# Two more early blocks, their stores on GpSimd's queue, and an operand loaded in two pieces

## The chip, the cores and the metric

The kernel runs on one core of a Trainium2 chip. The core has five engines with queues of their own: TensorE (PE in the profile; its weight loads are PEld), VectorE (DVE), ScalarE (ACT), GpSimd (POOL) and SyncE (SP). DMA transfers are issued by an engine's instruction, here mostly by SP, some by ACT and POOL, and are carried out by 16 DMA engines that all queues share. The metric is the time of one execution on the device in microseconds. The time before is 2615.43 us, the median of three runs.

## The reference

The kernel computes two things one after the other: a layer that mixes along the sequence by a Fourier transform, and a feed-forward layer on its result.

```python
X = np.fft.rfft(x, axis=1)                 # x: 8 x 3008 x 256
Yr = Xr @ w_r - Xi @ w_i + b_r
Yi = Xr @ w_i + Xi @ w_r + b_i
...                                        # soft threshold of Yr, Yi with 0.01
y = np.fft.irfft(Y, n=x.shape[1], axis=1)
...
h = y.reshape(24064, 256) @ w_in           # 256 x 2048
g = np.maximum(h, 0.0) ** 2
out = g @ w_out                            # 2048 x 256
```

## The kernel before

**Stages of the Fourier part.** 3008 is 64 x 47. Of each of the 8 batches, stage one transforms along the 47 in 13 blocks (J = 13): a block of 120 x 512 numbers of x is loaded, multiplied by constant matrices, copied from PSUM by ScalarE and stored in a scratch tensor `s1[b]` in HBM. Stage two reads `s1[b]` in 24 groups, transforms along the 64, mixes by w_r and w_i, applies the threshold, transforms back along the 64 and stores into `s3[b]`. The last stage (class `Back`) transforms back along the 47: it reads `s3[b]` in 16 groups per batch. Its operand is the tile `du`, 128 partitions x 3 x 256 numbers. Slots 0 and 1 are two columns of the first 128 rows of `s3[b]`; slot 2 holds on its lower and its upper 64 partitions the same two columns of the last 64 rows. `Back.mm` (lines 461, 464 and 465) multiplies slot 0, slot 1 and slot 2, in this order, for each half of 128 channels.

**Two phases.** In the first phase ("front") the first batch is done in full fp32 (`Fwd32`, `Unit32`), while the weights w_in and w_out are loaded and split into a high and a low part on VectorE, ScalarE and GpSimd. The second phase ("main") runs the feed-forward layer in steps of a tile's 500 or 504 tokens and 256 hidden units (class `Step`, line 484; psh and pso are its PSUM tiles): 7 products of a Strassen scheme on 128 x 250 tiles in three passes, the square of the positive part, a split, and 12 products with w_out. Between the steps' products the stages of later batches are spread by a list of jobs with due times in half steps, 96 to a batch (`fwd_tasks`, `pair_tasks`, `back_tasks`): the main phase of batch b also computes stage one of batch b + 2, stage two of batch b + 1 and the last stage for the next tile.

**The second batch** has no main phase ahead of it in which its stage one could run. The first `PRE` of its 13 blocks (class `Fwd2`, matmuls at line 352) are done at the end of the front: `load_early` issues their loads on SP, each behind the load of a stage two group, into buffers `x6`; after the last group `run` makes eight matmul passes, ScalarE copies 120 x 512 numbers to a buffer of tag `xf` (three of them), and the block is stored. Before, `PRE` is 5, and these stores are issued by ScalarE (line 225 on ACT). The other blocks run as jobs of the first main phase: the next two are loaded before its first step and due at 0.5 and 1.4, the rest at distances of 0.9; they are stored by SP. Stage two of the second batch is due from 10.6 on.

**What sets the order.** A planner orders each engine's instructions by its own estimate of times. `load_next` (line 108) chains all loads of the main phase in the order of the program on SP (and those of `kcm` on POOL). At the start of main the order is: the `du` loads of the first three groups, two weight loads (line 139), two `xt` loads for the next blocks of the second batch. The first three groups borrow the three `mc` buffers for `du`; all others share one buffer of tag `du`, so the load of a group can't start before the group ahead has been multiplied. The first tile's operands `yt` are made by VectorE and ScalarE out of the three groups' results (`dy`, `yr`, `ms`), and the main products (psh) need them.

Of the kernel before, what the change touches and what calls it, by code (L numbers as in the profile page):

```python
# [9 lines left out]
F32 = mybir.dt.float32  # L10
# [13 lines left out]
B, S, D, FF = 8, 3008, 256, 2048  # L24
N1, N2, G = 64, 47, 24
NP = N1 // 2
# [7 lines left out]
NP1 = N1 + 1  # L34
FRONT = {
    "a32": 1, "b32": 1, "w320": 1, "w321": 1, "big": 4, "small": 4, "ds": 1, "dw": 3, "ka": 5, "xe": 7,
    "kv": 3, "psf": 6, "x6": 5, "xf": 3, "nam": 1,
}
MAIN = {
    "xs": 1, "xe": 1, "du": 1, "kv": 1, "kp": 1, "kq": 1, "ksh": 1, "ksl": 1, "kxl": 1, "kb": 1, "yr": 1,  # L40
# [18 lines left out]
def fnet_moe(ctx: ExitStack, tc, x, w_r, w_i, b_r, b_i, w_in, w_out, bm, cm, dx, a32, c32, out):  # L59
    nc = tc.nc  # L60
    pe, act, dve, pool = nc.tensor, nc.scalar, nc.vector, nc.gpsimd
# [5 lines left out]
    s3 = [dram.tile([M2 + M2, NP, D], F32, name=f"s3_{b}") for b in range(B)]  # L67
# [13 lines left out]
    def memory(stack, name, **kwargs):  # L81
        return stack.enter_context(tc.tile_pool(name=name, bufs=2, reuse_waits="tile", **kwargs))
# [5 lines left out]
    def T(name, shape, dt, tag=None):  # L88
        tag = tag or name
        return pools.get(tag, phase["pool"]).tile(shape, dt, name=name, tag=tag, bufs=phase["bufs"].get(tag, 2))  # L90

    def bank(shape, name="psf"):
        return phase["psum"].tile(shape, F32, name=name, tag=name, bufs=phase["bufs"].get(name, 1))

    def copy(eng, out, in_):
        if eng is act:
            return act.copy(out=out, in_=in_)  # L97
        return eng.tensor_copy(out=out, in_=in_)  # L98
# [7 lines left out]
    def load_next(out, in_, eng=nc.sync):  # L106
        with tc.issue_after(chain[eng].ins):
            chain[eng] = eng.dma_start(out, in_)
# [24 lines left out]
    class Double:  # L133
# [3 lines left out]
        def load(self):  # L137
            self.st = T("dst", [128, 512, 2], I32, tag="big")
            self.get = nc.sync.dma_start(self.ins(self.st), self.src)
# [64 lines left out]
    class Fwd:  # L204
# [28 lines left out]
        def run(self):  # L233
            ps = bank([128, 2, D])
            for t in range(2):
                nc.tensor.matmul(ps[:M1, t], am32[:, t], self.u[:, t], start=True, stop=True)  # L236
            self.ev = T("xe", [M1, 1, 2, D], F32)
            copy(act, self.ev[:, 0], ps[:M1])
            self.store()
# [99 lines left out]
    class Fwd2(Fwd):  # L339
# [8 lines left out]
        def run(self):  # L348
            ps = bank([128, 2, D])
            for t in range(2):  # L350
                for i in range(2):
                    nc.tensor.matmul(
                        ps[:M1, t], nam if t and i else am32[:, t], self.xt[:, 0, i], start=i == 0, stop=i == 1
                    )
            self.ev = T("xe", [M1, 1, 2, D], F32, tag="xe" if self.q >= PRE else "xf")
            copy(act, self.ev[:, 0], ps[:M1])
            self.store(nc.sync if self.q >= PRE else act)

# [78 lines left out]
    class Back:  # L439
# [8 lines left out]
        def load(self):  # L448
            self.u = T("du", [128, 3, D], F32R, tag="du" if self.spans[0][0] else "mc")
            ps = slice(2 * self.q, 2 * self.q + 2)  # L450
            load_next(self.u[:, :2].bitcast(F32), s3[self.b][:128, ps])
            for p in range(2):
                load_next(self.u[64 * p:64 * p + 64, 2].bitcast(F32), s3[self.b][128:, 2 * self.q + p])

        def mm(self):
            self.y = y = T("dy", [128, 2, W2], F32)
# [190 lines left out]
    def convert(n, after=None):  # L647
        p = parts[n]
        p.bits(after)
        p.join()  # L650
        if n % 4 > 1:
            p.split()
        elif n % 4:
            win_sums(n // 4, parts[n - 1:n + 1])
# [8 lines left out]
    paced = [(n, 2 * (n - EARLY)) for n in range(EARLY, len(parts) - LATE)]  # L663
    loads = [(k - 1, parts[n]) for n, k in paced] + [(20 + j, p) for j, p in enumerate(parts[-LATE:-2])]

    PRE = 5
    nam = T("nam", [M1, M1], F32)
    act.mul(nam, am32[:, 1], -1.0)
    second = [Fwd2(1, q) for q in range(J)]
    for r in range(-5, len(units) + 3):  # L670
# [10 lines left out]
        while loads and loads[0][0] <= r:  # L681
            p = loads.pop(0)[1]
            with tc.issue_after((units[r + 5] if r + 5 < len(units) else units[-1]).get.ins):
                p.load()
        for n, k in paced:
            if k + 3 == r:
                convert(n, units[k])
        if 0 <= r - 12 < PRE:
            second[r - 12].load_early(units[min(r + 5, len(units) - 1)].get)
    for q in range(PRE):  # L690
        second[q].run()
# [3 lines left out]
        pool=memory(ctx, "main"), bufs={**{k: FRONT[k] for k in CONV}, **MAIN, "psf": 2}, psum=memory(ctx, "main_ps", space=PSUM)  # L695
# [16 lines left out]
    nam = T("nam", [M1, M1], F32)  # L712
    act.mul(nam, am32[:, 1], -1.0)
    for q in range(PRE, PRE + 2):
        second[q].load()
    jobs = []
    for m in range(2 * len(steps) + 4):
        b, r = divmod(m, slots)
        if r == 0 and b < B:
            jobs = [(t - slots, job) for t, job in jobs]  # L720
            if b + 1 < B:
                first, step, end = 1.0, 6.1, 7.1
                if b == 0:
                    first, step, end = 11.2, 5.3, 9.1
                    for q in range(PRE, J):
                        if q > PRE + 1:
# [112 lines left out]
```

## Time and profile before

| | |
|---|---|
| median of 3 runs | 2615.43 us |
| lowest and highest run | 2613.71 and 2618.53 us |
| the profiled execution | 2614.82 us, of which the span of its instructions is 2613.1 us |
| mean granted TensorE clock | 0.995 |
| TensorE busy | 2564.3 us, 98% of the span |
| matmuls of the steps (L484) | 1176.2 us (pso) and 1072.9 us (psh) |
| moved through DMA | 250.51 MB, 95 GB/s of HBM traffic over the span |

All numbers of the profile are of one execution. A row of the timeline gives the start and the length in microseconds, the engine, the line of the kernel, the operation, the tile written and the tiles read, and how many instructions are merged in the row; a bracket holds the idle time of the engine just before and what ended it. Rows with an engine name and q (SPq, ACTq, POOLq) are DMA issues: their time is that of the issue, and the transfer lands later. In the list of transfers a row gives the target and the source, the queue, the count, the size of one and the median time from issue to landing.

### The profile page before, as it was taken

To read this page: it belongs to the slowest core of one execution; us is meant where nothing else is said; L and a number is where in the kernel's file an instruction comes from. 1 tells how busy PE (TensorE), PEld (TensorE's weight loads), DVE (VectorE), ACT (ScalarE), POOL (GpSimd) and SP (SyncE) were. 2 spreads that over 40 slices of the span, in tenths; PEclk is the share of its full clock that TensorE was granted. 3 is DMA by queue.
4 is the path that set the end of the run, shared out by engine and by line. 5 is a ranking of instruction groups with operands and counts; after the bars stand their busy time and mean duration, and the time that the engine had idled before them with its cause. 6 is when DMAs were issued, how large, how long until landed. Compare 5 with 4: busy or idle time off the path is not lost.

```text
span 2613.1 us, 47540 instructions
## 1 busy us (share of the span) xinstructions
PE 2564.3 (98%) x16908; PEld 2347.0 (90%) x16908; DVE 1782.3 (68%) x3797; ACT 1672.7 (64%) x2434; POOL 1657.0 (63%) x1628
## 2 busy tenths in 40 slices
PE   6799999999999999999999999999999999999999
PEld 4689989999999999999999999999999999999998
DVE  6877766667767767577676776667676677765554
ACT  3556656666666666666666666666666666666665
POOL 2246666766766667667666676666667666666564
PEclk8999999999999999999999999999999999999999
DMA  8733332333332332233332333323332223221100
GB/s 267 236 110 110 102 113 82 95 106 107 95 91 75 116 104 86 84 95 113 104 92 82 97 110 100 99 76 101 103 108 80 71 79 101 71 65 41 33 17 17
DMA packets 191455, 250.51 MB, mean 96 GB/s; under 512 B 21755, under 2 KB 135923, under 8 KB 191219
## 3 DMA queue, kind: packets, MB, share of 16 engines
q1 hardware_dynamic: 178240, 223.89, 28.1%
q0 software_dynamic: 12304, 22.35, 3.6%
q8 instruction: 136, 2.23, 0.4%
q10 hardware_dynamic: 675, 1.23, 0.2%
q14 instruction: 100, 0.82, 0.1%
HBM read 146.85 MB, written 100.53 MB: 95 GB/s over the span
## 4 chain that ended last, share of the span: by engine, by line
PE 84%; POOL 1%; DMA 1%; issue 0%; DVE 0%; ACT 0%; POOLq 0%; SPq 0%; ACTq 0%; DVEq 0%
PE pso L484 36%; PE psh L484 32%; PE psf L301 6%; PE psf L280 2%; PE psf L236 2%; PE psf L333 2%; PE psf L464 1%; PE psf L465 1%; PE psf L461 1%; DMA du<-s 1%; POOL mg L101 0%; POOL yt L101 0%; POOL ms L101 0%; POOL ms L500 0%; ACT mc L484 0%
## 5 line engine op out<-in xcount | busy, mean ns | idle before, releaser
L101 POOL TENSOR_TENSOR mg<-mc,mg 128x500 fp32r<-128x500 f32 (+1 forms) x768 | 975.0, 1290 | 594.3 <-ACT mg L97 549.7
L484 PE MATMUL pso<-mg,wout 128*128 128x500 f32 (+1 forms) x4608 | 1176.2, 392 | 1.8 <-ACT mg L97 1.3
L484 PE MATMUL psh<-yt,win 128*128 128x250 f32 (+1 forms) x8064 | 1072.9, 281 | 1.5 <-DVE mc L484 1.2
L484 ACT ACTIVATE mc<-mc 128x1000 f32<-128x1000 f32 (+1 forms) x768 | 802.6, 1045 | 406.6 <-DVE mc L484 397.3
L484 PEld LDWEIGHTS psh<-yt,win 128*128 128x128 f32 x8064 | 1022.2, 189 | 34.3 <-PE psh L484 1.9
L484 PEld LDWEIGHTS pso<-mg,wout 128*128 128x128 f32 x4608 | 818.7, 189 | 130.0 <-POOL mg L101 1.9
L484 DVE TENSOR_TENSOR mc<-psh,mv 128x500 f32<-128x500 f32 (+3 forms) x768 | 419.1, 547 | 428.1 <-PE psh L484 395.4
L97 ACT CAST mg<-mc 128x1000 fp32r<-128x1000 f32 (+1 forms) x384 | 396.9, 1034 | 18.4 <-ACT mc L484 0.4
L484 DVE TENSOR_TENSOR mv<-psh,mu 128x500 f32<-128x500 f32 (+1 forms) x384 | 260.6, 679 | 53.5 <-PE psh L484 21.8
L301 PE MATMUL psf<-wx,kxh 128*128 128x256 f32 x1008 | 206.7, 281 | 2.4 <-ACT kxh L97 1.7
L98 DVE COPY mp<-psh 128x250 f32<-128x250 f32 (+1 forms) x384 | 159.7, 416 | 39.2 <-PE psh L484 16.2
L301 PEld LDWEIGHTS psf<-wx,kxh 128*128 128x128 f32 x1008 | 166.3, 189 | 6.7 <-ACT kxh L97 1.9
L101 POOL TENSOR_TENSOR ksl<-kv,ksh 128x512 fp32r<-128x512 f32 x84 | 108.8, 1295 | 94.6 <-ACT ksh L97 94.5
L484 DVE TENSOR_TENSOR mu<-psh,mp 128x250 f32<-128x250 f32 (+1 forms) x384 | 160.5, 418 | 11.5
L215 POOL TENSOR_TENSOR xs<-xt 120x256 f32<-120x256 f32 x156 | 115.4, 760 | 72.5 <-DMA xt<-x_in 67.6
L484 DVE TENSOR_TENSOR mc<-psh,mp 128x250 f32<-128x250 f32 (+1 forms) x384 | 156.8, 408 | 4.3 <-PE psh L484 2.8
L322 DVE TENSOR_TENSOR kv<-psf,ke 64x256 f32<-64x256 f32 x336 | 141.8, 422 | 22.9 <-PE psf L301 14.2
L301 PE MATMUL psf<-wx,kxl 128*128 128x256 f32 x504 | 141.1, 280 | 1.0 <-DVE kxl L101 1.0
L97 ACT COPY dy<-psf 128x188 f32<-128x188 f32 x256 | 76.9, 313 | 82.7 <-PE psf L465 82.2
L313 DVE TENSOR_TENSOR ke<-psf,bias 128x512 f32<-128x512 f32 x84 | 58.0, 691 | 102.0 <-PE psf L301 101.9
L97 ACT CAST ksh<-kv 128x512 fp32r<-128x512 f32 x84 | 52.0, 619 | 114.3 <-DVE kv L101 113.4
L97 ACT CAST kuh<-psf 128x256 fp32r<-128x256 f32 x192 | 68.4, 372 | 88.2 <-PE psf L333 71.4
(102 smaller groups left out, 2565.4 us busy)
## 6 DMA issues: line engine op xcount, KB each, us to landing
du<-s SPq DMA_DIRECT2D x128, 256.0 KB, 2.9
s<-kuh SPq DMA_DIRECT2D x192, 128.0 KB, 1.8
s<-kul SPq DMA_DIRECT2D x192, 128.0 KB, 1.8
kcm<-cm_in POOLq DMA_DIRECT2D x84, 256.0 KB, 3.3
ka<-s SPq DMA_DIRECT2D x84, 256.0 KB, 3.4
s<-xe SPq DMA_DIRECT2D x87, 240.0 KB, 2.4
xt<-x_in SPq DMA_DIRECT2D x86, 240.0 KB, 3.3
du<-s SPq DMA_DIRECT2D x256, 64.0 KB, 2.8
```

What stands on the lines that cost most here:

```text
L97: return act.copy(out=out, in_=in_)
L98: return eng.tensor_copy(out=out, in_=in_)
L101: return eng.tensor_tensor(out=out, in0=a, in1=b, op=ALU.subtract)
L215: return eng.tensor_tensor(out=out[:, :n], in0=self.xt[:, :n, 0], in1=self.xt[:, :n, 1], op=(ALU.add, ALU.subtract)[t])
L236: nc.tensor.matmul(ps[:M1, t], am32[:, t], self.u[:, t], start=True, stop=True)
L280: nc.tensor.matmul(pv[:, :, c, g, :], self.a[:, g, c * 128:(c + 1) * 128], bg, start=True, stop=True)
L301: self.last = nc.tensor.matmul(ps, l, wx[j][:, k, c, :], start=n == 0, stop=n == 5)
L313: dve.tensor_add(out=self.e, in0=self.pe, in1=bias)
L322: dve.tensor_add(out=v[64 * r:64 * r + 64, g], in0=ps[gs], in1=self.e[gs, r])
L333: nc.tensor.matmul(ps[:, :D], self.cm[:, g, j * 128:(j + 1) * 128], r[:, g], start=n == 0, stop=n == 2)
L461: mm = nc.tensor.matmul(pv[:, :, 0], self.u[:, 0, cs], dx_sb[:, 0], start=True, stop=False)
L484: last_of[eng] = op(*args, **kwargs)
```

## The change

It has three parts. `PRE` becomes 7, with 7 buffers of tag `x6`: blocks 5 and 6 of the second batch move from the main phase to the end of the front. Their place at the start of main, with the loads ahead of the first step, is taken by blocks 7 and 8, and the jobs of blocks 9 to 12 come two places (1.8) earlier. The stores of the early blocks are issued by GpSimd's queue. And slot 2 of `du` is loaded by one transfer of 128 partitions instead of two of 64: its HBM side is written by hand as 2 x 64 x 256 numbers (two columns, 64 rows, 256 channels), its SBUF side stays 128 x 256.

```diff
 FRONT = {
     "a32": 1, "b32": 1, "w320": 1, "w321": 1, "big": 4, "small": 4, "ds": 1, "dw": 3, "ka": 5, "xe": 7,
-    "kv": 3, "psf": 6, "x6": 5, "xf": 3, "nam": 1,
+    "kv": 3, "psf": 6, "x6": 7, "xf": 3, "nam": 1,
 }
...
             copy(act, self.ev[:, 0], ps[:M1])
-            self.store(nc.sync if self.q >= PRE else act)
+            self.store(nc.sync if self.q >= PRE else pool)
...
             load_next(self.u[:, :2].bitcast(F32), s3[self.b][:128, ps])
-            for p in range(2):
-                load_next(self.u[64 * p:64 * p + 64, 2].bitcast(F32), s3[self.b][128:, 2 * self.q + p])
+            l = s3[self.b][128:, ps]
+            l = bass.AP(tensor=l.tensor, offset=l.offset, ap=[[D, 2], [NP * D, 64], [1, D]])
+            load_next(self.u[:, 2].bitcast(F32), l)
...
-    PRE = 5
+    PRE = 7
```

## The prediction

> **What bounds the kernel now.** I read the page first, then the busy time by stretches, then the order of time around the change, the queue's own waits and the transfers.
>
> ```profile
> PE 2564.3 (98%) x16908; PEld 2347.0 (90%) x16908; DVE 1782.3 (68%) x3797; ACT 1672.7 (64%) x2434; POOL 1657.0 (63%) x1628
> ...
> 100.00:120.00 20.00, 18.28 (x90) 15.39 (x88) 15.13 (x34) 10.02 (x24) 3.63 (x5) 1.00 0.65 211
> 120.00:140.00 20.00, 12.59 (x63) 10.76 (x63) 10.65 (x26) 5.77 (x15) 0.28 (x1) 0.74 0.58 178
> ...
> 500.00:1000.00 500.00, 499.85 (x3376) 461.48 (x3376) 349.50 (x746) 325.59 (x474) 339.87 (x341) 1.00 0.34 100
> ...
>   DMA du<-s: 5.2, 10
> ```
>
> The rows with a colon are stretches: length, then busy time of PE, its weight loads, DVE, ACT and POOL, granted clock, DMA share, GB/s. From 500 us on TensorE is busy 499.85 of 500 us: any matmul taken out there is a gain of its own length, and any wait put in front of a matmul is a loss of its own length. The one stretch near the change with room is 120 to 140 us: 12.59 of 20 us, at a clock of 0.74. The last row (from the view of the tile du) says that TensorE now loses only 5.2 us in all, ten times, to late du, the operand whose load is changed. So there is nothing to win for du after the start-up, only something to lose.
>
> The transition, in order of time (start, length, engine, line, work):
>
> ```profile
> 113.55 10.21 SPq L108 DMA_DIRECT2D du<-s  x9
> 113.59 0.59 PE L352 MATMUL psf<-x,nam 120*120 120x256 f32 x2
> 115.31 0.59 PE L352 MATMUL psf<-x,nam 120*120 120x256 f32 x2
> 118.77 0.59 PE L352 MATMUL psf<-x,nam 120*120 120x256 f32 x2
> 119.01 0.44 PE L461 MATMUL psf<-dx_sb,du 128*128 128x188 f32 x1
> 121.87 0.51 ACT L97 COPY dy<-psf 128x188 f32<-128x188 f32 x2
> 122.61 0.36 PE L461 MATMUL psf<-dx_sb,du 128*128 128x188 f32 x1 [2.60 <-DVE yr L471]
> 123.49 0.53 ACT L97 COPY dy<-psf 128x188 f32<-128x188 f32 x2 [1.10 <-PE psf L465]
> 125.00 9.72 SPq L108 DMA_DIRECT2D xt<-x_in  x3
> 125.53 0.49 PE L465 MATMUL psf<-dx_sb,du 128*128 128x188 f32 x1 [0.70 <-DMA du<-s]
> 129.16 1.44 DVE L101 TENSOR_TENSOR yt<-ms,yt 128x504 fp32r<-128x504 f32 x2
> 130.63 2.89 PE L352 MATMUL psf<-xt,am 120*120 120x256 f32 x6 [3.27 <-DVE yt L101]
> 136.11 2.44 PE L484 MATMUL psh<-yt,win 128*128 128x252 f32 x18
> ...
> SPq L108 <- DMA s<-xe: 6.0, 5, 2.5
> ```
>
> Five early blocks (L352) run back to back, one each 1.72 us (113.59 to 115.31). Then come the first three du groups (119.01, 122.61, 125.53), the chain to yt (until 130.60), and two more blocks of the second batch, which hold the main products up until 136.11. The nine du issues take 10.21 us although an issue takes about 0.5 us. The last row, from the waits of SP's queue, says why: five waits on stores s<-xe, one for each early block. These loads read another tensor, so it isn't the data they wait for; I read it as completion counters shared by SP's and ACT's transfers.
>
> **Part 1, two more early blocks.** In the front they add 2 x 1.72 = 3.4 us of TensorE behind 118.77, so the first du group moves from 119.0 to 122.5 us. That hurts less than it looks: its copy dy ran only at 121.87, behind weight conversion on ACT and DVE. With dy at about 123.2 and the spacing of the rows (dy to the next group 0.74 us, dy to dy 1.62 us), the third group would end near 126.6, where it ends now (125.53 plus two more matmul pairs). Late in the transition, two blocks (now numbers 7 and 8) still stand in front of the main products; two later ones disappear from slots where TensorE is full: -3.4 us. Two more 240 KB loads go into the front at a time of busy DMA: 480 KB at the 211 GB/s of the first row above is 2.3 us of transfer; most of it lies beside other work, and I charge 0.7 us, between nothing and 2.3.
>
> **Part 2, the stores on GpSimd's queue.** ACT loses five issues of 0.3 us, worth nothing. The five SP waits (6.0 us) go, so SP can issue all du loads, the weight loads behind them and the first two xt loads (125.00 now) some 6 us sooner. Then blocks 7 and 8 have their data before yt is ready and run in TensorE's idle time from 126.6 to 130.6. The main products would start at about 130.8 and not at 136.11: -5.3 us. With a GpSimd store
>
> ```profile
> kcm<-cm_in POOLq DMA_DIRECT2D x84, 256.0 KB, 3.3
> s<-xe ACTq DMA_DIRECT2D x5, 240.0 KB, 2.9
> b<-b_i_in POOLq DMA_DIRECT2D x1, 64.0 KB, 6.6
> ```
>
> (last number: median us from issue to landing) the third buffer comes round after 3 x 1.72 = 5.2 us, so 3.3 us hides; at the 6.6 us of the front's row the copies of blocks 4 and 7 would be late and hold ACT, up to 4 us of that gain. I take 3.3. Parts 1 and 2 with all transfers in time: -3.4 - 5.3 + 0.7 = **-8 us**.
>
> **Part 3, du in two pieces.** It saves 128 issues of 0.49 us on SP, which hides under TensorE anyway: nothing. But the new piece is of a new kind. Both 64-row pieces have 64 rows of 1 KB on both sides. The merged one has 128 partitions on the SBUF side, and on the HBM side 2 x 64 rows, two strides that can't be joined. What does a queue do with that?
>
> ```profile
> DMA packets 191455, 250.51 MB, mean 96 GB/s; under 512 B 21755, under 2 KB 135923, under 8 KB 191219
> q1 hardware_dynamic: 178240, 223.89, 28.1%
> du<-s SPq DMA_DIRECT2D x128, 256.0 KB, 2.9
> s<-xe SPq DMA_DIRECT2D x87, 240.0 KB, 2.4
> xt<-x_in SPq DMA_DIRECT2D x86, 240.0 KB, 3.3
> du<-s SPq DMA_DIRECT2D x256, 64.0 KB, 2.8
> x<-x_in SPq DMA_DIRECT2D x6, 480.0 KB, 7.4
> s<-xe SPq DMA_DIRECT2D x6, 480.0 KB, 6.8
> x<-x_in SPq DMA_DIRECT2D x6, 240.0 KB, 5.3
> am<-a_in SPq DMA_DIRECT2D x1, 112.5 KB, 2.1
> ```
>
> The list of transfers has 28 rows (du x128 is the first, b<-b_i x1 above the last) with 1372 issues. 16 small packets for each would be 21952; there are 21755, 197 fewer. The transfers of 120 rows are 87 + 86 + 6 + 6 + 6 + 5 (the ACT row above) + 1 = 197. So each transfer ends with one small packet per DMA engine that it used, 16 of them where its rows are 64 or 128, and 15 where they are 120: the number of engines divides the rows. No transfer here has a first dimension of two on one side. If the number must divide the first dimension of both sides, it is 2 for the merged piece. I take this: it is the same rule carried to the new shape, while an even spread would need the queue to join strides that don't join.
>
> [...]
>
> The price: 223.89 MB in 28.1% of 16 x 2613.1 us is 19.1 KB per us of one engine. An engine now moves 4 KB of a small piece, then 64 KB: 60 KB more, 61440 / 19060 = 3.2 us. Landing goes from 2.8 to **6.0 us** after issue (an even spread would leave it near 2.9; these are the two ends). Since the piece is issued one issue (1.47 / 3 = 0.49 us) after the first, it lands 6.5 us after the first. When is it needed? By L465, the third matmul of a group; examples of the three tighter kinds, issue and use:
>
> ```profile
> 1059.88 1.47 SPq L108 DMA_DIRECT2D du<-s  x3
> 1064.87 0.36 PE L465 MATMUL psf<-dx_sb,du 128*128 128x188 f32 x2
> 1065.26 1.46 SPq L108 DMA_DIRECT2D du<-s  x3
> 1070.92 0.27 PE L465 MATMUL psf<-dx_sb,du 128*128 128x188 f32 x1
> 1112.59 1.46 SPq L108 DMA_DIRECT2D du<-s  x3
> 1119.88 0.27 PE L465 MATMUL psf<-dx_sb,du 128*128 128x188 f32 x1
> ```
>
> Of the 16 groups of that batch one has 4.99 us, four have 5.7 (as at 1065.26), three 7.1 to 7.3, eight 8.6 and more. The waits are 6.5 - 5.0 = 1.5 and 4 x 0.8 = 3.2, together 4.7 us a batch, 8 batches: **+38 us**, on an engine without idle time to give, since a load starts only when the group before has left its single buffer. Behind L465 in TensorE's order stand the main products, and behind those DVE, ACT and GpSimd.
>
> It also eats into the front. Three first pieces (16 KB an engine) and three merged ones (64 KB) behind each other on two engines take 3 x 80 / 19 = 12.6 us; from about 115 us the third lands near 128, against L465 at 125.53 now. yt is then ready near 133, the main products start there: -3 us in place of -5.3. Parts 1 and 2 give -3.4 - 3 + 0.7 = -6 us.
>
> **Sum.** The profiled execution took 2614.8 us (span 2613.1 and 1.7 around it), 0.6 under the median of the runs. 2614.8 - 6 + 38 = 2647 us. A measurement can tell about 0.2%, 5.2 us.
>
> **Rivals.**
> - *The merged piece spreads over 16 engines* (or nearly so). For it: the SBUF side does have 128 rows, and ka<-s with 128 rows shows nothing odd. Then only -8 us is left: 2607 us. Chance 0.13.
> - *Two engines, but in time.* If it lands 4.7 us after issue (two engines at a better pace), only the 4.99 us group waits, by 0.2 us: 2 us in all, and 2611; at 5.2 us after issue the waits are 0.7 and nothing: 6 us, 2615 us. From 5.2 us on the four groups of 5.7 us join, and each 0.1 us more costs 8 x 0.5 us: this decides the sign. Chance 0.10.
> - *Two engines and worse.* Other SP transfers queue behind the 64 KB on these two engines (xt follows du by 1.5 us), and two groups whose L465 now stands 4 us behind L461 may be put closer, since one transfer fewer looks earlier to the planner: 1 to 3 us a batch more and a slower landing of 6.75 us, near 2690 us or above. Chance 0.06.
>
> **How the numbers follow.** My forecast has 0.71. Its own spread, landing 5.4 to 6.75 us, is +10 to +75 us. The range is 2612 to 2692: it leaves out the first rival and the far end of the third. Slower by over 0.2%: 0.71 + 0.06 = 0.77. Within: the second rival and a little of the first, 0.11. Faster: 0.12.
>
> **What would show it.** The du row of 128 transfers of 128 KB with a landing near 6 us and not 2.8; small packets down: 1372 - 128 issues, with 2 and not 16 for the merged ones; TensorE's wait on du<-s near 40 us and not 5.2, most of it before L465; no SP waits on s<-xe around 115 us; L352 on xt before 130 us. A landing near 3 us would make the whole price of part 3 wrong, and the time would be under 2610 us. If du lands late but TensorE waits little, the planner has moved the groups, and the step on slack is the wrong one.

## The result and the profile after

| | before | after |
|---|---|---|
| median of the runs | 2616.98 us (4 runs) | 2718.84 us (4 runs) |
| lowest and highest | 2613.71 to 2618.68 us | 2716.82 to 2720.52 us |
| span of the profiled execution | 2613.1 us | 2718.8 us |
| mean granted TensorE clock | 0.995 | 0.988 |

After over before is 1.0388, with a 95% interval of 1.0375 to 1.0400: 102 us slower. The forecast was 2647 us, in a range of 2612 to 2692. The direction was right. The loss is more than three times the one forecast: 2647 us is 32 us above the 2614.8 us from which the forecast counted.

The page of the kernel after, its first part, its packets and the chain that ended last:

```profile
span 2718.8 us, 47264 instructions
...
PE 2597.4 (96%) x16908; PEld 2362.8 (87%) x16908; DVE 1791.1 (66%) x3797; ACT 1677.6 (62%) x2434; POOL 1657.3 (61%) x1635
...
DMA packets 187228, 250.47 MB, mean 92 GB/s; under 512 B 17950, under 2 KB 132118, under 8 KB 186994
...
PE 65%; DMA 13%; POOL 2%; DVE 2%; issue 2%; ACT 2%; SPq 1%; POOLq 0%; ACTq 0%; DVEq 0%
PE pso L485 27%; PE psh L485 24%; DMA du<-s 12%; PE psf L301 5%; PE psf L280 2%; PE psf L236 2%; PE psf L333 2%; PE psf L466 1%; POOL mg L101 1%; SPq L108 1%; ACT mc L485 1%; DVE mc L485 1%; PE psf L465 1%; DMA s<-xe 1%; ACT mg L97 0%
```

TensorE executes the same 16908 matmuls, but the chain that sets the end now runs through transfers for 13% of the span, 12% through du alone. The small packets answer the question of the width. With two engines for the merged piece they should number (1244 - 128) x 16 + 128 x 2 - 197 = 17915; the page has 17950, and the 35 more are five for each of the seven stores that GpSimd's queue now carries. With 16 engines for each piece it would be 19707.

The busy time by stretches of 500 us, the row of the slot 2 products among TensorE's groups (busy us, mean ns of one, idle us before them), and TensorE's wait on du (us, times, the longest; line numbers are one higher than before from the edit on, so L466 is the old L465 and L485 the old L484):

```profile
500.00:1000.00 500.00, 484.23 (x3233) 443.95 (x3232) 336.84 (x716) 313.10 (x454) 320.94 (x322) 1.00 0.32 93
1000.00:1500.00 500.00, 484.85 (x3197) 443.15 (x3197) 325.81 (x693) 313.54 (x450) 318.89 (x319) 0.99 0.32 92
1500.00:2000.00 500.00, 488.00 (x3264) 448.17 (x3263) 333.84 (x717) 316.62 (x460) 325.13 (x324) 1.00 0.33 95
2000.00:2500.00 500.00, 483.06 (x3209) 441.49 (x3208) 328.00 (x705) 315.32 (x444) 309.74 (x298) 1.00 0.24 73
...
L466 PE MATMUL psf<-dx_sb,du 128*128 128x188 f32 x256 | 72.9, 298 | 71.4 <-DMA du<-s 71.0
...
PE psf L466 <- DMA du<-s: 71.0, 56, 4.1
```

Before, TensorE was busy 499.6 to 499.9 us of each stretch; now it loses 12 to 17 us in every one. The loss isn't in the start-up but everywhere that `du` is loaded. 71.0 of the 71.4 us of idle time before the slot 2 products wait for du, 56 times, and before the change du cost 5.2 us in all.

Three groups that follow each other near 1100 us show such waits from issue to use (timeline):

```profile
1095.63 0.88 SPq L108 DMA_DIRECT2D du<-s  x2
1102.57 0.35 PE L466 MATMUL psf<-dx_sb,du 128*128 128x188 f32 x1 [1.74 <-DMA du<-s]
1103.29 0.89 SPq L108 DMA_DIRECT2D du<-s  x2
1110.24 0.39 PE L466 MATMUL psf<-dx_sb,du 128*128 128x188 f32 x2
1110.66 0.87 SPq L108 DMA_DIRECT2D du<-s  x2
1117.90 0.47 PE L466 MATMUL psf<-dx_sb,du 128*128 128x188 f32 x2 [1.67 <-DMA du<-s]
```

The landing of the merged piece is read from its waits. It is the second issue of each pair, about 0.4 us after the row's start. In the first group it was there 6.6 us after its issue, in the third 6.9. Over the 54 groups of the main phase that wait, the time from its issue to the end of the wait is 5.4 to 7.1 us, with a median of 6.3. A piece that lands late is more likely to be waited for, so this is a little high: by the completion events in the trace the median of all 128 merged pieces is 6.1 us (the forecast took 6.0).

The transition after the change:

```profile
111.95 6.12 SPq L108 DMA_DIRECT2D du<-s  x6
118.17 5.05 SPq L139 DMA_DIRECT2D dst<-w_out_in  x2
120.32 0.59 ACT L97 COPY xe<-psf 120x512 f32<-120x512 f32 x1 [3.63 <-DMA s<-xe]
123.32 14.73 SPq L108 DMA_DIRECT2D xt<-x_in  x3
130.63 0.53 PE L466 MATMUL psf<-dx_sb,du 128*128 128x188 f32 x1 [4.05 <-DMA du<-s]
133.95 2.89 PE L352 MATMUL psf<-xt,am 120*120 120x256 f32 x6 [1.46 <-DVE ms L501]
139.31 2.46 PE L485 MATMUL psh<-yt,win 128*128 128x252 f32 x18
```

The third group waits 4.05 us for its merged piece, ScalarE waits 3.63 us for a store of GpSimd's queue, and the main products start at 139.31, 3.2 us later than before (136.11), though the waits of SP on the stores of xe are gone.

### The profile page after: what moved, and what is told of

It is laid out like the page before. It is cut to its first block, busy times and chain, and to the rows that moved or that the text cites. A ratio compares the mean times of both kernels' runs of the same rounds, so it can differ in the third digit from the quotient of the medians.

```text
span 2718.8 us, 47264 instructions
## 1 busy us (share of the span) xinstructions
PE 2597.4 (96%) x16908; PEld 2362.8 (87%) x16908; DVE 1791.1 (66%) x3797; ACT 1677.6 (62%) x2434; POOL 1657.3 (61%) x1635
## 2 busy tenths in 40 slices
DMA packets 187228, 250.47 MB, mean 92 GB/s; under 512 B 17950, under 2 KB 132118, under 8 KB 186994
## 4 chain that ended last, share of the span: by engine, by line
PE 65%; DMA 13%; POOL 2%; DVE 2%; issue 2%; ACT 2%; SPq 1%; POOLq 0%; ACTq 0%; DVEq 0%
PE pso L485 27%; PE psh L485 24%; DMA du<-s 12%; PE psf L301 5%; PE psf L280 2%; PE psf L236 2%; PE psf L333 2%; PE psf L466 1%; POOL mg L101 1%; SPq L108 1%; ACT mc L485 1%; DVE mc L485 1%; PE psf L465 1%; DMA s<-xe 1%; ACT mg L97 0%
## 5 line engine op out<-in xcount | busy, mean ns | idle before, releaser
L485 PE MATMUL pso<-mg,wout 128*128 128x500 f32 (+1 forms) x4608 | 1179.1, 393 | 6.1 <-POOL mg L101 4.1
L485 PE MATMUL psh<-yt,win 128*128 128x250 f32 (+1 forms) x8064 | 1079.5, 282 | 1.0 <-DVE mu L485 0.9
L485 ACT ACTIVATE mc<-mc 128x1000 f32<-128x1000 f32 (+1 forms) x768 | 803.2, 1046 | 440.7 <-DVE mc L485 431.9
L485 PEld LDWEIGHTS psh<-yt,win 128*128 128x128 f32 x8064 | 1029.4, 190 | 32.4 <-DVE mu L485 1.1
L485 PEld LDWEIGHTS pso<-mg,wout 128*128 128x128 f32 x4608 | 820.9, 189 | 143.3 <-POOL mg L101 14.4
L485 DVE TENSOR_TENSOR mc<-psh,mv 128x500 f32<-128x500 f32 (+3 forms) x768 | 419.1, 548 | 414.9 <-PE psh L485 380.7
L485 DVE TENSOR_TENSOR mv<-psh,mu 128x500 f32<-128x500 f32 (+1 forms) x384 | 260.8, 679 | 55.6 <-PE psh L485 23.8
L215 POOL TENSOR_TENSOR xs<-xt 120x256 f32<-120x256 f32 x156 | 112.8, 744 | 185.0 <-DMA xt<-x_in 124.9
L485 DVE TENSOR_TENSOR mu<-psh,mp 128x250 f32<-128x250 f32 (+1 forms) x384 | 160.6, 418 | 11.3
L485 DVE TENSOR_TENSOR mc<-psh,mp 128x250 f32<-128x250 f32 (+1 forms) x384 | 157.2, 409 | 16.3 <-PE psh L485 15.6
L472 DVE TENSOR_TENSOR yr<-psf,dy 128x188 f32<-128x188 f32 (+4 forms) x256 | 78.8, 313 | 128.2 <-ACT dy L97 125.4
L466 PE MATMUL psf<-dx_sb,du 128*128 128x188 f32 x256 | 72.9, 298 | 71.4 <-DMA du<-s 71.0
```

The costliest lines, as they stand in the source:

```text
L215: return eng.tensor_tensor(out=out[:, :n], in0=self.xt[:, :n, 0], in1=self.xt[:, :n, 1], op=(ALU.add, ALU.subtract)[t])
L466: nc.tensor.matmul(ps[:, 0], self.u[:, 2, cs], dx_sb[:, 1], start=False, stop=True)
L472: dve.tensor_add(out=o, in0=ps[:, 0, lo:hi], in1=y[:, c, lo:hi])
L485: last_of[eng] = op(*args, **kwargs)
```

## The experiments

Two theories to start with. **Width:** the merged piece is carried by two DMA engines, lands late, and TensorE waits for it. **Planner:** the change lets the planner choose another order of instructions, and the order is what costs. A third question was what parts 1 and 2, the blocks and the stores, bring by themselves (the expectations call it the **front** theory where it is to explain the loss). Behind each measured time stands its ratio to the kernel before on the same chip, with the 95% interval. A span is about 1.8 us shorter than the time of its run in all of them.

### One part alone

The kernel before with nothing but the merged piece:

```diff
-            for p in range(2):
-                load_next(self.u[64 * p:64 * p + 64, 2].bitcast(F32), s3[self.b][128:, 2 * self.q + p])
+            l = s3[self.b][128:, ps]
+            l = bass.AP(tensor=l.tensor, offset=l.offset, ap=[[D, 2], [NP * D, 64], [1, D]])
+            load_next(self.u[:, 2].bitcast(F32), l)
```

> The kernel before with the two-piece du alone: 5 early blocks, their stores on ScalarE's queue. Width theory (the merged piece is moved by two DMA engines and lands some 6.2 us after its issue): the whole loss is here, 2705 to 2728 us, TensorE waiting 60 to 75 us on du before L465. Front theory (a good part of the 102 us comes from the two more early blocks and GpSimd's stores): clearly less than the change, under 2670 us. Planner theory (the loss is the closer order that the planner gives to L465 with one transfer fewer): as the width theory here.

Measured: 2713.62 us, 1.0367 (1.0353 to 1.0382). TensorE's waits for du before L466 are 70.1 us in 64 places. The whole loss is part 3.

The kernel after with the three pieces of before (parts 1 and 2 alone; the reverse edit):

> The changed kernel with the three-piece du put back: seven early blocks, stores on GpSimd's queue. Width theory: a small gain, 2605 to 2613 us, no waits on du in the steady part. Front theory: over 2650 us. Planner theory: 2605 to 2613 us.

Measured: 2613.07 us, 0.9981 (0.9972 to 0.9990), 4.8 us under the 2617.9 of its kernel before. The sign of -8 us was right, its size wasn't quite.

### The same order, another width

The merged piece is walked row by row instead of column by column: 64 x 2 x 256 on the HBM side. To match, the rows of the constant dx are interleaved.

```diff
-            l = bass.AP(tensor=l.tensor, offset=l.offset, ap=[[D, 2], [NP * D, 64], [1, D]])
+            l = bass.AP(tensor=l.tensor, offset=l.offset, ap=[[NP * D, 64], [D, 2], [1, D]])
...
-    dx[:64, 1, :w], dx[64:, 1, w:] = h[:64], h[:64]
+    dx[0::2, 1, :w], dx[1::2, 1, w:] = h[:64], h[:64]
```

> The changed kernel with du still in two pieces, but the HBM side of the merged one walked as 64 x 2 x 256 and not 2 x 64 x 256 (its first dimension is 64); the rows of the constant matrix dx are interleaved to match. Bytes, rows and number of transfers stay. Width theory: 16 engines again, landing near 3 us, small packets 16 for each of these transfers, 2603 to 2612 us. Planner theory: the order is that of the changed kernel, so the loss stays: over 2650 us. Front theory: over 2650 us.

Measured: 2624.45 us, 1.0026 (1.0017 to 1.0035). On every engine the instructions stand in the same order as in the kernel after; nothing differs but how the piece is walked. So the order by itself can't be what costs the 94 us between the two.

From its page, its groups, its list of transfers and its timeline (the first and the third of the three groups above):

```profile
span 2622.7 us, 47264 instructions
...
PE 2568.8 (98%) x16908; PEld 2348.8 (90%) x16908; DVE 1785.5 (68%) x3797; ACT 1673.1 (64%) x2434; POOL 1661.6 (63%) x1635
...
DMA packets 189020, 250.48 MB, mean 96 GB/s; under 512 B 19742, under 2 KB 133910, under 8 KB 188786
...
L466 PE MATMUL psf<-dx_sb,du 128*128 128x188 f32 x256 | 67.3, 276 | 0.8 <-DMA du<-s 0.8
...
du<-s SPq DMA_DIRECT2D x128, 128.0 KB, 2.8
...
1057.26 0.89 SPq L108 DMA_DIRECT2D du<-s  x2
1062.58 0.27 PE L466 MATMUL psf<-dx_sb,du 128*128 128x188 f32 x1
...
1069.06 0.88 SPq L108 DMA_DIRECT2D du<-s  x2
1074.47 0.38 PE L466 MATMUL psf<-dx_sb,du 128*128 128x188 f32 x2
```

The small packets are 19742 = 1244 x 16 - 197 + 35: 16 per piece now. The piece lands after 2.8 us and nothing waits for it. The first of the groups uses it 5.3 us after its first issue, where two engines made it 6.9.

As the order is the same, the two traces can be laid side by side instruction by instruction, and one can see where the kernel after falls behind. Of the 96 us between the spans, 81 arise at L466 (60 products at which the lag grows by more than 0.15 us), 12 at the products of the steps and 3 at the first two xt blocks. The 81 are the 71 us of waits and 10 more: in the spread version these 60 products start before the one ahead of them has ended, by 9.5 us in all, and behind a wait this overlap is lost. Of the 12, 9 lie in six stretches at half clock, shown in the last section.

Transfers that are issued right behind the merged piece are late too, as the third rival of the prediction had it. By the completion events the loads of `xt` land 5.9 us after their issue at the median and not 3.8, and GpSimd's waits for them grow from 97.5 to 124.9 us. TensorE hardly feels it: the products of the later blocks (line 236) fall behind by nothing, and only the first two blocks by the 3 us.

The kernel before with this spread piece and nothing else:

> The kernel before with the two-piece du of first dimension 64 alone. Width theory: within 4 us of the kernel before (2612 to 2620), since the saved issues hide. Planner theory: over 2650 us. Front theory: as the kernel before.

Measured: 2620.20 us, 1.0007 (0.9998 to 1.0016). Its order is that of the first experiment on every engine, and again only the width differs: 93 us. So two pieces in place of three bring nothing measurable even when the merged one is as fast as the small ones.

### Where the lead between load and use comes from

The kernel after, and each group's products due half a half step (1.6 us) later:

```diff
-            jobs += [(at, k.load), (at + 1.6, k.mm)]
+            jobs += [(at, k.load), (at + 2.1, k.mm)]
```

> The kernel after (merged piece on two engines) with each group's products due 2.1 and not 1.6 half steps behind its load: 0.5 of about 3.2 us, so some 1.6 us more between load and use. Width theory: the merged piece still lands 6.2 us after issue, but most of TensorE's 71 us of waits before the slot 2 product were only 0.7 to 1.7 us long, so they fall to 10 to 30 us and the half-clock windows with them: 2625 to 2665 us. Rival (the loss isn't the lead but what 64 KB on two engines does to the other transfers): the waits move to others, time above 2690 us.

Measured: 2710.34 us, 1.0357 (1.0343 to 1.0371). Nearly nothing was gained, 8 of 102 us: the waits for du before L466 are still

```profile
PE psf L466 <- DMA du<-s: 63.8, 59, 4.3
```

Both theories missed: the waits neither shrank by much, as the one had it, nor moved elsewhere, as the other had it. A job's due time orders the program; when a product then stands in TensorE's order is the planner's choice, and it again puts many of them some 5 us behind the first issue: in this order, run with a piece on 16 engines (next section), 40 of the 128 groups use slot 2 within 5.5 us of the first issue, against 44 without the later due time. So the lead has to be changed where it is made. The same kernel, on two engines still, but slot 2 in a tile `dv` of its own with two buffers, loaded first:

```diff
-    "xs": 1, "xe": 1, "du": 1, ...
+    "xs": 1, "xe": 1, "du": 1, "dv": 2, ...
...
-            self.u = T("du", [128, 3, D], F32R, tag="du" if self.spans[0][0] else "mc")
+            self.u = T("du", [128, 2, D], F32R, tag="du" if self.spans[0][0] else "mc")
+            self.v = T("dv", [128, D], F32R)
...
+            load_next(self.v.bitcast(F32), l)
+            load_next(self.u.bitcast(F32), s3[self.b][:128, ps])
...
-                nc.tensor.matmul(ps[:, 0], self.u[:, 2, cs], dx_sb[:, 1], start=False, stop=True)
+                nc.tensor.matmul(ps[:, 0], self.v[:, cs], dx_sb[:, 1], start=False, stop=True)
```

> The merged piece stays 2 x 64 x 256 on two engines, but slot 2 becomes a tile of its own (dv) with two buffers, and its load is issued ahead of that of slots 0 and 1: it no longer has to wait until the group before has been multiplied. If the loss is landing time (6.2 us) against a lead that the single buffer keeps short, most of the waits before the slot 2 product go: 71 us of waits to under 30, 2615 to 2660 us. If the planner puts the product at its own estimate of the landing again, whatever the buffers, the waits stay and the time with them: above 2690 us.

Measured: 2640.69 us, 1.0095 (1.0080 to 1.0111): 78 of the 102 us are back. Its groups (L467 is the slot 2 product, L463 the first one) and an example of issue and use:

```profile
L467 PE MATMUL psf<-dx_sb,dv 128*128 128x188 f32 x256 | 70.9, 277 | 0.0
L463 PE MATMUL psf<-dx_sb,du 128*128 128x188 f32 x256 | 67.7, 265 | 21.3 <-DMA du<-s 11.2 <-ACT xe L97 7.5 <-DVE yr L473 2.5
...
1067.26 0.52 SPq L108 DMA_DIRECT2D dv<-s  x1
...
1079.16 0.27 PE L467 MATMUL psf<-dx_sb,dv 128*128 128x188 f32 x1
```

No product waits for slot 2 any more; the shortest time from issue to use is 7.0 us, in the example it is 11.9. What is left is mostly waits of the first product, 11.2 us on the piece that is now issued behind it and 7.5 us on copies in and just after the transition. The piece on two engines is slow (6.1 us in the kernel after), but most of the slowness was paid only because load and use stood so close. The edit does two things, a second buffer and another order of the two loads, and they were not tried apart.

### The rest between the spread piece and three pieces

The spread version is 11 us slower than three pieces with the same blocks and stores, which the width theory had not expected. The later due time was tried on both:

> The same order of instructions on every engine as the run with later use, but the merged piece walked row by row (64 x 2 x 256), which spreads over 16 engines and landed in 2.8 us. The difference to the run with later use is what the width still costs at this lead: 10 to 50 us by the width theory. If the 9 to 12 us by which the first spread version was slower than three pieces are a cost of the spread piece itself, this is again 8 to 12 us above the three pieces with later use; if they came from the order that the planner happened to choose, the two differ by under 8 us, of either sign.

> Seven early blocks, stores on GpSimd, three pieces, products due 2.1 half steps behind the load. Nothing waited for du in the version with 1.6 (waits under 1 us in all), so more lead has nothing to win: 2608 to 2622 us, the differences being those of another order.

Measured: 2620.23 us (1.0011, 1.0002 to 1.0020) with the spread piece, 2626.08 us (1.0037, 1.0023 to 1.0051) with three pieces, above the 2608 to 2622 us expected. The sign has turned: the spread piece is now 6 us the faster one. And the three pieces alone went from 2613 to 2626 us by a later due time, with the same work and 0.3 us of waits for du. So orders that the planner makes of the same work differ by up to 13 us, half a per cent, and the 11 us are the order's rather than a cost of the spread piece (which, alone in the kernel before, cost nothing measurable either). Which waits of an order make the difference was not taken apart further.

### The blocks and the stores

Part 1 alone (seven early blocks, stores on ScalarE) and part 2 alone (five, stores on GpSimd), both with three pieces. The first as an edit of parts 1 and 2; the second is the opposite line in the kernel before:

```diff
-            self.store(nc.sync if self.q >= PRE else pool)
+            self.store(nc.sync if self.q >= PRE else act)
```

> Part 1 alone: seven early blocks, stores on ScalarE's queue, three pieces. By the prediction's steps -3.4 + 0.7 = -2.7 us, with the main products starting no earlier: 2612 to 2615 us. If the waits of SP's queue on the stores grow from five to seven and delay the xt loads, nothing is left: 2615 to 2619 us.

> Part 2 alone: five early blocks, stores on GpSimd's queue, three pieces. By the prediction's steps -5.3 us: 2610 to 2613 us. If the landing of GpSimd's stores (5.2 us and not 3.3) holds the copies and the first du group, the gain is under 3 us: 2614 to 2618 us.

Measured: part 1 alone 2615.95 us, 0.9996 (0.9987 to 1.0005); part 2 alone 2614.23 us, 0.9991 (0.9982 to 1.0000). The intervals of both reach to no change at all. With part 1 alone it went as the second half of its expectation has it: SP waits on seven stores, 8.8 us in all and not 6.0, xt is issued at 127.22, and the main products start at 138.16, 2 us later than before. Part 2 alone lies in the range of the second half of its expectation, but for another reason. Its transition (timeline):

```profile
111.72 5.06 SPq L108 DMA_DIRECT2D du<-s  x9
116.89 1.08 SPq L139 DMA_DIRECT2D dst<-w_out_in  x2
118.21 14.23 SPq L108 DMA_DIRECT2D xt<-x_in  x3
126.46 1.45 DVE L101 TENSOR_TENSOR yt<-ms,yt 128x504 fp32r<-128x504 f32 x2
128.34 2.88 PE L352 MATMUL psf<-xt,am 120*120 120x256 f32 x6 [3.70 <-DMA xt<-x_in]
133.96 2.45 PE L484 MATMUL psh<-yt,win 128*128 128x252 f32 x18
```

The nine du issues take 5.06 us and not 10.21: the waits of SP on the stores are gone, as forecast, and xt is issued at 118.21 and not at 125.00. But it isn't there before 128.34, 10 us after its issue, behind two transfers of 512 KB for the weights. So the blocks wait for xt (3.70 us) where they waited for yt before, and the main products start 2.2 us sooner instead of 5.3.

That reading has a test: both parts, and the two xt loads issued ahead of the two weight loads.

```diff
+        for q in range(PRE, PRE + 2) if name == "load" else ():
+            second[q].load()
         for p in parts[-2:] if name == "load" else ():
...
-    for q in range(PRE, PRE + 2):
-        second[q].load()
```

> Seven early blocks, stores on GpSimd, three pieces, and the first two xt loads issued ahead of the two weight loads (dst) and not behind them. In the runs with GpSimd stores the xt loads were issued 6 to 7 us sooner than before but landed only after 10 us, behind the weight loads. If that landing is what is missing of the predicted 8 us, xt lands within 6 us of issue, the two blocks run while yt is made and the main products start 2 to 4 us sooner than at 135.0: 2608 to 2611 us. If the order on TensorE keeps the blocks behind yt, or the du loads hold yt, nothing changes: 2612 to 2615 us.

Measured: 2610.75 us, 0.9977 (0.9968 to 0.9986).

```profile
117.66 1.07 SPq L108 DMA_DIRECT2D xt<-x_in  x2
119.00 1.00 SPq L139 DMA_DIRECT2D dst<-w_out_in  x2
127.48 2.37 PE L352 MATMUL psf<-xt,am 120*120 120x256 f32 x6
129.49 1.45 DVE L101 TENSOR_TENSOR yt<-ms,yt 128x504 fp32r<-128x504 f32 x2
130.12 1.46 PE L352 MATMUL psf<-xt,am 120*120 120x256 f32 x6
131.66 2.44 PE L484 MATMUL psh<-yt,win 128*128 128x252 f32 x18
```

Now xt lands 5.8 and 6.2 us after its issue, the blocks run while yt is made, and the main products start at 131.66. This is the fastest of all kernels that were run, though its interval overlaps that of parts 1 and 2 alone.

The other suspect was the buffers of tag xf: GpSimd's stores land after 5.2 us (with seven blocks and three pieces), and ScalarE waits for them. Parts 1 and 2 with four buffers and not three:

```diff
-    "kv": 3, "psf": 6, "x6": 7, "xf": 3, "nam": 1,
+    "kv": 3, "psf": 6, "x6": 7, "xf": 4, "nam": 1,
```

> Seven early blocks, stores on GpSimd, three pieces, and four instead of three buffers of tag xf. With three, ScalarE waits 1.4 + 1.9 + 0.8 us for the stores (landing 5.2 us against 3 x 1.72 us), and the first du group's copy stands behind that. If this is what is left of the predicted 8 us (4.8 came), the main products start 1 to 3 us sooner: 2609 to 2612 us, against 2613 with three buffers. If the loads of du or xt end the wait by then, no change: 2612 to 2615 us.

Measured: 2614.03 us, 0.9987 (0.9978 to 0.9996), no faster than three buffers. The copies of the early blocks no longer wait for stores, but the main products start at 136.23, because their blocks wait 3.95 us for yt. The buffers weren't the limit.

Start of the main products and two blocks fewer (3.4 us by the rows, not measured alone) give these kernels to about 1 us, but for the last. As each time is uncertain by some 2.4 us, the table fits this account without proving it:

| kernel | main products start | against 136.11 | two blocks fewer | sum | measured against before |
|---|---|---|---|---|---|
| part 2 alone | 133.96 | -2.2 | 0 | -2.2 | -2.1 |
| part 1 alone | 138.16 | +2.1 | -3.4 | -1.4 | -0.4 |
| parts 1 and 2 | 135.04 | -1.1 | -3.4 | -4.5 | -4.8 |
| the same, four xf buffers | 136.23 | +0.1 | -3.4 | -3.3 | -2.7 |
| the same, xt first | 131.66 | -4.5 | -3.4 | -7.9 | -5.5 |

## Why the prediction was right and wrong

**Two engines: right.** The number of engines was read from the count of small packets, and that count has now been seen with 2 (17950) and with 16 (19742) for the same bytes. The difference is that of 128 pieces with 14 engines fewer each: they make 1792 packets, and 19742 - 17950 = 1792. The packets themselves show it too: in the trace of the kernel after, the merged piece issued at 465.78 us moves as two series of 1 KB packets, in each of them one about every 42 ns, and each series ends with one small packet, 4.8 and 5.3 us after the issue. That an even spread would need the queue to join strides was the author's assumption; the counts show two engines, and no run shows why.

**Landing at 6.0 us: right.** Measured 6.1 us at the median of all pieces and 6.3 of those that were waited for, against 2.8 us on 16 engines: 3.3 us more, where 3.2 had been worked out.

**The waits, 4.7 us a batch and 38 us in all: the step that failed, and its mechanism was right.** It was a sum over the 16 groups of one batch, times 8, at before's places of the products. Counted in the traces over all 128 groups, a group waits for as long as its slot 2 product would start ahead of the landing, both counted from the first issue:

| order of which kernel | landing after first issue | sum of the waits |
|---|---|---|
| before, the batch quoted, times 8 | 6.5 us | 38 us |
| before, all batches | 6.5 us | 51 us |
| spread piece (the order of after) | 6.5 us | 68 us |
| the same, each piece with its own landing in the kernel after | 6.5 us at the median | 76 us |
| measured lag at L466 | | 81 us |

So 13 us come from taking one batch for all: its 4.8 us is the lowest sum that a batch of before has, three more have the same, and the other four have 5.9 to 8.8. 17 us came from the order: with one transfer fewer the planner puts the products closer (44 groups under 5.5 us from the first issue, before 22). In the batch quoted it moved above all the two groups that the third rival had named, from 10.0 and 8.6 us to 5.3 each. 8 us came from the scatter of the landings, 5.3 to 7.0 us after issue in the main phase and up to 14 in the transition; a single figure stood for all. The last 5 us of the lag are not taken apart. The planner's move had been given a chance of 0.06 and 1 to 3 us a batch; it was 2.1 us, and should have stood in the forecast itself: "near 2690 us or above" is the rival that came, if not with its landing of 6.75 us. The spread of +10 to +75 us comes out as +13 to +69 by the forecast's own steps.

**What the sum left out.** 12 us on the steps' products, which no step had; 9 of them are TensorE's half clock behind the waits.

**Parts 1 and 2, -8 us with all transfers in time:** -4.8 measured. The end of SP's waits (du issued in 5.1 us) came as forecast, and the two blocks (-3.4) fit the table. The reading of these waits as shared completion counters fits the trace of before: the five stores use five of the eight semaphores of SP's transfers, and GpSimd's transfers have eight others. The step that failed is that "blocks 7 and 8 have their data before yt is ready": xt was issued early but landed after 10 us, behind the weight loads. With xt ahead of them the main products start at 131.66; the forecast had 130.8. GpSimd's stores landed after 5.8 us in the kernel after, not 3.3, nearer the upper end that had been named; ScalarE did wait for them, 3.63 us, but four buffers brought nothing (with three pieces).

**Parts 1 and 2 beside the merged piece, -6 us:** here they brought nothing. The third merged piece was to land near 128 us and the main products to start near 133; it landed at 130.6 and they started at 139.31, later than before. The kernel after is 5 us slower than the merged piece alone (2718.84 and 2713.62 us; the intervals of the two ratios overlap). In both the main products start near 139.5, so that only the two blocks should be left. The order of the two differs, and orders were seen to differ by more than that; the sign is not settled.

## What to carry to other kernels

Before two transfers are merged, look at the outermost dimension on both sides: two here meant two engines, 6.1 us in place of 2.8, and the same bytes walked 64 x 2 instead of 2 x 64 gave the 94 us back. Whether a slower transfer costs anything is decided by the slack of its tightest users over the whole run, after the change has reordered them; sum over all of them, and not over one typical batch. And a load that is issued sooner gained little here while larger loads stood ahead of it: with part 2 alone xt was issued 6.8 us sooner (118.21 and not 125.00) and was there 10 us later, behind two weight loads of 512 KB; issued ahead of them it took 5.8 and 6.2 us.

## What the runs showed of the hardware

**Six windows at half clock stand behind short stretches in which TensorE was busy 26 to 49% of the time.** The busy time around the first wait quoted above, in the kernel after (columns as in the stretches, PEclk the third from the right):

```profile
1100.60:1104.00 3.40, 1.66 (x12) 1.37 (x11) 0.69 (x2) 1.00 (x3) 2.45 (x2) 1.00 0.09 30
1104.00:1107.40 3.40, 3.40 (x18) 3.40 (x17) 1.84 (x4) 1.60 (x2) 0.00 (x0) 0.50 0.53 143
1107.40:1110.00 2.60, 2.60 (x15) 2.21 (x14) 1.16 (x3) 1.50 (x2) 0.21 (x1) 0.99 0.18 65
```

1.5 us after the wait of 1.74 us has ended, TensorE runs for 3.4 us at half its clock. From 400 us to the last 50 us the kernel after has six such windows, the spread version one. Each of the six begins within 1.7 us of the end of a wait of 1.7 to 2.5 us, but other waits of 1.5 to 2.4 us had none. The trace shows what tells them apart. The other five begin 49, 189, 289, 337 and 577 times 3.413 us after the first, so all lie on one grid of 3.413 us. Cut by that grid, the six pieces just ahead of them are those in which TensorE was least busy from 400 us on, 26 to 49% of the time (1.66 of 3.40 us in the first row); the next ones, from 49% up, have no half clock behind them. A wait of 2.37 us near 808 us fell across two pieces of the grid and cost no clock. The one window of the spread version (between 400 and 600 us, where its mean clock was 0.99 and not 1.00) has 2.05 of 3.40 us busy ahead of it and no wait over 0.8 us, so the bound isn't exact. Inside the six windows the steps' products fall behind by 9 us of their 12.

**Stores of GpSimd's queue** landed after 4.1 to 6.3 us here (medians of the ten runs that have them), the same stores on ScalarE's queue after 2.7 to 3.4 us (medians of the three runs without a piece on two engines). The queue isn't the only difference: with GpSimd's stores the loads of du and of the weights run beside them instead of behind them, and in the kernel before with nothing but the merged piece the last four of ScalarE's five stores took 5.4 to 6.8 us too: the second, issued at 114.17, held a copy until 121.00.
